# Block-sparse attention into a gated feed-forward: common keys of two query blocks in one 64-column product, two units to a batch, and batch loads issued by GpSimd

## The chip, the cores and the metric

The kernel runs on one core of a Trainium2 chip. The metric is the device time of one execution in microseconds (us), smaller is better. Before the change, three runs took 306.48, 301.97 and 305.78 us; the median is 305.78 us.

The engines are named as the profile names them: PE is TensorE (matrix products), PEld its weight loads, DVE is VectorE, ACT ScalarE, POOL GpSimd, SP SyncE (which only issues DMAs here). SPq and POOLq are their instruction queues.

## The reference: what is computed

Four batches, eight heads, 768 positions, head dimension 64. The positions form 24 blocks of 32. A query block attends to itself and its two neighbours, to the first and the last block, and to three blocks drawn by a table; the first and the last query block attend to everything. The result goes, 512 wide, through a root-mean-square norm and a gated feed-forward of inner width 1536:

```python
mask = np.abs(blk_i - blk_j) <= window              # window = 1, blocks of 32
mask = mask | (blk_i == 0) | (blk_j == 0) | (blk_i == n_blocks - 1) | (blk_j == n_blocks - 1)
for qb in range(n_blocks):
    for kb in sampled_blocks[qb]:
        mask[qb * block:(qb + 1) * block, kb * block:(kb + 1) * block] = True
scores = np.where(mask, scale * q @ k.T, -1e9)
attn = softmax(scores)                              # over the keys
x = (attn @ v), heads side by side                  # 3072 x 512
xn = x / sqrt(mean(x * x) + 1e-6) * rms_g
out = (silu(xn @ w_gate) * (xn @ w_val)) @ w_out    # 512 -> 1536 -> 512
```

## The kernel before

**Tiles and units.** The 3072 rows are 24 tiles of 128 rows, six to a batch. The first batch is computed densely (all 768 keys for every query, with the mask added through 24 more rows of the contraction: `dk`, `dexp`, `dav`). The other three batches are sparse: a tile is four query blocks of 32, and of each block only the keys that it attends to are gathered. Tile 5 (`AT`) of a sparse batch holds the first and the last block, which attend to everything, and two ordinary blocks. The tiles of a batch are grouped into units (`UNITS`, L63, from `SPLIT`, L62): a unit goes through the feed-forward together, with 128 columns for each of its tiles. Batch 0 has units of 1, 1, 1 and 3 tiles, batch 1 of 1, 2, 1, 2, batch 2 of 1, 2, 3, and batch 3 of 3, 3; these are 13 units.

**A sparse batch.** K, Q and V come in from DRAM as float32, in two halves of 768 KB each (`load_kv`, L439-444), into one of three raw buffers (`RAWS`, pool `raw`). They are cast to bfloat16 (`fill_k`, `fill_v`, on whichever of POOL, DVE, ACT the planner takes from `CE`, L819), K and Q are transposed by PE (`turn`, L464) and copied out by ACT (`turned`). V is stored to a table of rows in DRAM (`store_v`, L473), and the blocks that a tile needs are read back from it: fixed ones by SP (`pair_v`, L533-541), sampled ones, whose addresses are in registers, by SP for two of the three draws and by POOL for the third (`block_v`, L517). Sampled blocks of K are copied within the chip (`kg_sampled`, L507, by POOL; its time stands at L153, 198 copies).

Of a tile, four heads at a time (a "run"), PE computes scores (`qk`, L562, in row tiles of 64 x 128; `qka`, L578, for tile 5), ACT the exponential (L568, L585), PE the product of probabilities and V (`av`, matmul at L611), DVE the division by the sum, which is a 65th column of V (`xo`, L621-622).

**The product in question (`av`, L589-614).** The probabilities lie keys-by-queries, so they are the weights of the matmul, and 65 columns of V stream past. Keys come in groups of 128. For each head of an ordinary tile each of the four query blocks has 128 keys of its own (`vg[:, 0..3]`), and two neighbouring blocks share another 128 (`vg[:, 4]` and `vg[:, 5]`). Every product is 32 weight columns wide and stands in one of four column tiles of the array (`tile_position=(0, 32 * i)`, tile size 128 x 32), which write 32 partitions each. An ordinary run has 4 heads of 8 products, 32 in all. For tile 5 the first two blocks have six groups of 128 keys in common, and the other two have two groups each: 16 products a head, 64 a run. There are 30 ordinary runs and 6 runs of tile 5; this is 1344 products.

**After attention.** A sum of squares (`sq`, L638, DVE), the inverse root (`rsq`, L647-649, POOL), the scaling (`xq`, L656, DVE), a transposition: by PE and a copy for the first seven units (`tr` L667 and `cp`, `NPET` in L51), by a transposing DMA of SP for the rest (`xt`, L678). Then, in parts of 384 or 512 columns, gate product (`proj`, L691, G below), tanh (`th`, L700, ACT), DVE (`uu`, L706), value product (L691 with `wv`, V below), DVE (`hp`, L717), and at last the output product (`yy`, L730, Y below) with its copy (`yo`) and store (`so`).

**Weights and loads at the start.** The weights come by POOL's DMAs with a cast (`load_w` L254, `load_wo` L258), in four parts of gate and value and two of the output. The loads of batches 1 to 3 are issued by SP, in a fixed sequence; those of K of batch 1 wait in SP's queue until parts 2 and 3 of the value weights have landed (`gate_sync`, L261, called in `lkv`, L939).

**What sets the order.** All instructions are issued by a planner inside the kernel (L1154-1247): every operation has a cost on each engine that may do it, dependencies, buffers it takes and releases, and a priority; the planner steps through time, takes the operation that could start first, and writes it to its engine. Each engine executes its own list strictly in that order. So constants (`FP`, `KFP`, `KDP`, `SQP`, `CPV`, `DLAT`, and the lists of engines `CE`, `SQE`, `CPE`) change the order everywhere. The planner's cost of a run of `av` is 12 x 0.0315 us (L1017), 28 x 0.0315 us for tile 5.

Of the kernel before, what the change touches and what calls it, by code (L numbers as in the profile page):

```python
# [17 lines left out]
def kernel(  # L18
# [19 lines left out]
    P = 128  # L38
    B, H, S, D = q.shape
    NB = S // 32  # L40
    NC = S // P
# [10 lines left out]
    NSLOT, NAUG, NOPEN, NDB = 5, 2, 2, 1  # L52
    IXAT, RGAT = 36.0, 48.0
    NPT, NKG, NVG, NRAW = 5, 2, 4, 3
    AHEAD, HURRY, HURU = 0.2, ("av", "xo", "sq", "rsq", "xq", "tr", "cp"), 0
    NSTARV, ZPAT, NG2 = 3, 32.0, 20
    AH = {"uu": 0.3, "hp": 0.3, "th": 0.3}
    WARM = (11, 10, 2)
    HD, NT3 = NC * D // 2, 3
    VE = ("SP", "SP", "POOL")  # L60
    LP = {(x, b) for x in "" for b in (1, 2, 3)}
    SPLIT = (((5,), (0,1), (2,),( 3, 4)), ((5,), (0, 1), (2, 3, 4)), ((5, 0, 1), (2, 3, 4)))  # L62
    UNITS = [(0, 0, 1), (0, 1, 1), (0, 2, 1), (0, 3, 3)]  # L63
    ND = len(UNITS)
    for b in range(NDB, B):
# [103 lines left out]
    def idle(n, bk=7):  # L169
# [7 lines left out]
        out=kmask, in_=kmask, compare_op=ALU.is_ge, fill=0.0,  # L177
        base=0, pattern=[[1, NC], [-32, NB]], channel_multiplier=NC)
    nc.gpsimd.affine_select(
        out=kmask, in_=kmask, compare_op=ALU.is_ge, fill=0.0,  # L180
        base=31, pattern=[[-1, NC], [32, NB]], channel_multiplier=-NC)
    nc.gpsimd.affine_select(
        out=ident, in_=ident, compare_op=ALU.not_equal, fill=1.0,
        base=0, pattern=[[-1, P]], channel_multiplier=1)
    nc.gpsimd.affine_select(
        out=Bm, in_=Bm, compare_op=ALU.is_ge, fill=0.0,
        base=1, pattern=[[-1, 32]], channel_multiplier=1)
    nc.gpsimd.affine_select(
        out=Bm, in_=Bm, compare_op=ALU.is_ge, fill=0.0,
        base=1, pattern=[[1, 32]], channel_multiplier=-1)  # L190
    nc.gpsimd.affine_select(
        out=Bm, in_=Bm, compare_op=ALU.not_equal, fill=1.0,
# [13 lines left out]
    for t in aug:  # L206
# [7 lines left out]
        out=eq[0:NB], in0=jb[0:NB], in1=samp_f[0:NB].unsqueeze(2).to_broadcast([NB, NRND, 32]),  # L214
# [4 lines left out]
    for r in range(NRND):  # L219
        nc.vector.tensor_tensor(  # L220
            out=Bm[0:NB], in0=Bm[0:NB], in1=eq[0:NB, r], op=ALU.max)
    nc.vector.tensor_scalar(
        out=Bneg, in0=Bm, scalar1=-MASKV, scalar2=MASKV, op0=ALU.mult, op1=ALU.add)
    qm = PS[:, 2, 0:NC * NB].rearrange("p (c j) -> p c j", j=NB)
    for c in range(NC):
        nc.tensor.matmul(
            out=qm[:, c, :], lhsT=Kind[0:NB, c, :], rhs=Bneg[0:NB, 0:NB], start=True, stop=True)
# [3 lines left out]
        out=aug[0][:, 1, :, 0, 0:D], in_=A[0][:, 1, :, 0:D])  # L231
# [277 lines left out]
    globs, kglob, vaugs = {}, {}, {}  # L509
# [79 lines left out]
    def av(b, n, pp, bk):  # L589
        p_ = [pts.pop((b, n, 2 * pp + i)) for i in range(2)] if n == AT else pts.pop((b, n, pp))  # L590
        vg = vgs[b, n]
        o_ = PS[:, bk[0], 0:4 * (D + 1)].rearrange("p (a d) -> p a d", a=4)
        tiles["o", b, n, pp] = o_
        begun = set()
        for a in range(4):
            hd = slice((4 * pp + a) * (D + 1), (4 * pp + a + 1) * (D + 1))
            w = []
            if n == AT:
                p1 = p_[a // 2][:, a % 2]
                for m in range(NC):  # L600
                    w += [(i, p1[:, 64 * m + 32 * i:64 * m + 32 * i + 32], vaugs[b][:, m, 4 * pp + a, :]) for i in range(2)]
                    if m < 2:
                        lo = 64 * NC + 64 * m
                        w += [(i, p1[:, lo + 32 * (i - 2):lo + 32 * (i - 1)], vg[:, (i, 5)[m], hd]) for i in (2, 3)]
            else:
                p1 = p_[:, a % 2, a // 2]
                w += [(i, p1[:, 32 * i:32 * i + 32], vg[:, i, hd]) for i in range(4)]
                w += [(i, p1[:, P + 32 * i:P + 32 * i + 32], vg[:, 4 + i // 2, hd]) for i in range(4)]
            last = {i: k_ for k_, (i, _, _) in enumerate(w)}
            for k_, (i, l_, r_) in enumerate(w):  # L610
                nc.tensor.matmul(  # L611
                    out=o_[32 * i:32 * i + 32, a, :], lhsT=l_, rhs=r_, start=i not in begun, stop=k_ == last[i],
                    tile_position=(0, 32 * i), skip_group_check=True)
                begun.add(i)

    def xo(u, t, pp):
        b, ns, nt = UNITS[u]
# [154 lines left out]
    banks[2] = 5.1  # L772
    S_, S3, TP1 = [(0, 1), (2, 3)], [(0, 1), (2, 3), (4, 5)], [(6,), (5,), (4,)]
    LAT = {"PE": 0.2, "ACT": 0.16, "DVE": 0.08, "POOL": 0.1, "DMA": 1.9, "DMA2": 2.0, "SP": 2.0, "GD": 2.2, "GQ": 2.5}
    DLAT = {"turnk": 3.0, "turnq": 3.0, "st": 2.5, "l": 4.0, "lq": 4.0, "cp": 2.2, "pvi": 3.0, "gd": 2.2}
    ALT = {"g": [(6,)], "y": [(7,)], "av": [(6,)]}
    SPM, RING = 1.0, 6.0
    ops, end, made = [], {}, {}
# [24 lines left out]
    for g, i in ((2, 0), (2, 1), (3, 0), (3, 1), (0, 2), (1, 2), (2, 2), (3, 2)):  # L803
# [3 lines left out]
        out=gB, in_=moe_rms_g.unsqueeze(0).to_broadcast([P, DM])))  # L807
# [2 lines left out]
        load_q2()  # L810

    WOG, ORD = None, "vkq"
    FP, QP3, SQP = 0.5, 2.5, 0.4
    KDV, LIC, PLI = 0.48, 1.5, 0
    GVC, GVP, GWP, GPC = 0.46, 0.5, 3.5, 0.52
    CPV, CPK, KFP, KDP = 1, 1, 1.1, 1.1
    D_, A_, P_ = {"DVE": 0.62}, {"ACT": 0.86}, {"POOL": 1.0}
    DA_, DP_, AP_, DAP_ = {**D_, **A_}, {**D_, **P_}, {**A_, **P_}, {**D_, **A_, **P_}
    CE = {1: (DP_, DP_, DP_), 2: (P_, P_, P_), 3: (DAP_,DAP_,DAP_)}  # L819
    KFE, SQE, YOE = ("DVE",), ("DVE", ), ("DVE", "ACT")  # L820
    TTE, TTP = ("ACT",), -1
    KDE, CPE = ("POOL",), ("ACT",)
    prev = None
    for i in range(NWC + NOC):
        for m in range(2 if i < NWC else 1):
# [33 lines left out]
        out=aug[1][:, 1, :, :, D:KQ], in_=aug[0][:, 1, :, :, D:KQ]), at=5.1)  # L859
    for g in range(NP):  # L860
# [12 lines left out]
        for i in range(2):  # L873
            for n_, (es, lo, hi) in enumerate((KP, QP)[i][g == 0]):
                m_ = len(es) * (hi - lo)
                if i == 0:
                    pri = (-1, g, 0.5 + 0.1 * n_ + (g == 0 and lo == 3))
                else:
# [4 lines left out]
                   pri, lambda e, p, a=(g, i, es, lo, hi): tpx(*a, p),  # L883
# [6 lines left out]
                elif g == 0 and lo == 0:  # L890
                    de.update(ac)
                op(("ev",) + key[1:], de, [key], pri,
                   lambda e, p, a=(g, i, es, lo, hi): evx(*a, e), [], [(None, key)])
# [24 lines left out]
    for e_ in REGS:  # L918
        for part, (w_, lo, hi) in enumerate(REGS[e_]):
            op(("rg", e_, part), {e_: {"POOL": 2.7, "ACT": 2.0, "SP": 1.5, "DVE": 2.7}[e_]}, [("ix", 5)], (6, part),  # L920
               lambda e, p, a=(e_, part): table_regs(*a), at=RGAT + (7.0 * part if e_ == "ACT" else 0.0))
# [9 lines left out]
    for b in range(NDB, B):  # L931
        for i in (0, 1, 2):
            for hf in range(2):
                key = ("kvq"[i], b, hf)
                if key[:2] in LP:
                    continue
# [14 lines left out]
        for hf in range(2):  # L951
            for c in range(2):
                op(("sfv", b, hf, c), ce[0], [("l", "v", b, hf), ("on",) if b == NDB else ("on", 1)], (CPV, b, 0),
                   lambda e, p, a=(b, hf, c): fill_v(*a, e), [("va", b)], [("raw", ("v", b, hf))])
                for i, x in enumerate("kq"):
                    op((("sfk", "sfq")[i], b, hf, c), ce[1 + i], [("l", x, b, hf)] + (tp0[i] if b == NDB else []), (CPK, b, 1 + i),
                       lambda e, p, a=(b, x, hf, c): fill_k(*a, e), [(x + "row", b)], [("raw", (x, b, hf))])
        fv = [("sfv", b, hf, c) for hf in range(2) for c in range(2)]
        op(("st", b), {"SP": 0.8}, fv + [("lt",)], (-1, b), lambda e, p, b=b: store_v(b), d=2.6)
        for x in "kq":  # L960
            for j in range(2):
                op(("tt" + x, b, j), {"PE": 12 * 0.056}, [("sf" + x, b, j, c) for c in range(2)], (TTP, b, j),
                   lambda e, p, a=(b, x, j): turn(*a, p), [(S_, ("tt" + x, b, j)), (x.upper() + "T", b)], [(x + "row", b)])
                op(("turn" + x, b, j), pick_({"ACT": 2.75, "DVE": 2.75}, TTE), [("tt" + x, b, j)], (-0.5, b, j),
                   lambda e, p, a=(b, x, j): turned(*a, e), [], [(None, ("tt" + x, b, j))])
# [58 lines left out]
    for u, (b, c0, nt) in enumerate(UNITS):  # L1024
        w = nt * P
        if b < NDB:
            w, last = nt * P, c0 + nt == NC
            ng = NC // JT[nt]
            for pr in range(NP):
# [3 lines left out]
                for g in range(ng):  # L1033
# [12 lines left out]
                   lambda e, p, a=(u, pr): dav(*a, p), [([(7,)] + [(6,)] * (u < 3), ("o", u, pr)), ("xo", u)],  # L1046
# [4 lines left out]
                   lambda e, p, a=(u, pr): dxo(*a), [], [(None, ("o", u, pr))])  # L1051
# [13 lines left out]
        for t in range(nt):  # L1065
            op(("xq", u, t), {"DVE": 0.75}, [("rsq", u), ("lg",)], (SQP, u, t),
               lambda e, p, a=(u, t): xq(*a), [("xq", u)],
# [11 lines left out]
        for f in range(NF // fg):  # L1079
            n_ = fg * w  # L1080
            op(("g", u, f), {"PE": fg * NP * mm(w)}, [("cp", u), ("w", w_of[f])], (4, u, f, 1),
               lambda e, p, a=(u, f): proj(*a, wg, "gp", p), [([(4,)] + [(6,)] * (2 < u < NG2), ("g", u, f)), ("hp", HG[u])])
            op(("th", u, f), {"ACT": 0.12 + n_ / 1200.0}, [("g", u, f)], (FP, u, f),
               lambda e, p, a=(u, f): th(*a), [("th", (u, f))])
            op(("uu", u, f), {"DVE": 0.155 + n_ / 960.0}, [("th", u, f)], (FP, u, f),
               lambda e, p, a=(u, f): uu(*a), [("uu", (u, f))],
               [(None, ("g", u, f)), ("th", (u, f))])
            op(("v", u, f), {"PE": fg * NP * mm(w)}, [("g", u, f)], (4, u, f, 0),
               lambda e, p, a=(u, f): proj(*a, wv, "vp", p), [([(5,)], ("v", u, f))],
               [("xn", u)] if f == NF // fg - 1 else [])  # L1090
            op(("hp", u, f), {"DVE": 0.155 + n_ / 960.0}, [("uu", u, f), ("v", u, f)], (FP, u, f),
               lambda e, p, a=(u, f): hp(*a), [],
               [(None, ("v", u, f)), ("uu", (u, f))])
        for t in range(nt):
            nh = 2 if u == NU - 1 and t == nt - 1 else 1
            for h in range(nh):
                for k_ in range(4):
# [3 lines left out]
                       lambda e, p, a=(u, t, 4 * h + k_): yy(*a, p),  # L1101
# [3 lines left out]
                   lambda e, p, a=(u, t, h): yo(*a, e), [("yo", (u, t, h))], [(None, ("y", u, t, h))])  # L1105
                op(("so", u, t, h), {"SP": 0.5 if b < NDB or c0[t] != AT else 1.5}, [("yo", u, t, h)], (0, u, t),
                   lambda e, p, a=(u, t, h): so(*a), [], [("yo", (u, t, h))], d=0.8 / nh)
# [46 lines left out]
    while ready:  # L1154
        pick = None
        for o in ready:
# [8 lines left out]
            for e in o["engs"]:  # L1165
                t1 = max(got[0] + (SPM if e == "SP" and o["key"] not in in_seq0 else 0.0), free[e])
                k_ = o["key"]
# [9 lines left out]
        _, o, e, t1, got = pick  # L1177
# [17 lines left out]
        k_ = o["key"]  # L1195
# [82 lines left out]
```

## Time and profile before

| | |
|---|---|
| profiled execution: its own time | 302.08 us |
| its span, first to last instruction | 300.5 us |
| granted TensorE clock, mean | 0.988 |
| PE busy | 279.2 us, 4605 matmul records |
| DVE, ACT, POOL busy | 203.6, 170.5, 134.3 us |
| DMA moved | 47.94 MB, mean 160 GB/s |

The profile gives, of one execution, the busy time of each engine, the chain of work that ended last (followed back from the last instruction: at each step to what released it), groups of instructions by source line, and the waits. A timeline view merges neighbouring instructions of one kind: start, time from the first start to the last end, what, and how many. PE's matmuls are pipelined, so the ends overlap the next start; the pace of PE is read from start to start. Some matmul records are missing (the products of L611 have 1312 records of 1344).

### The profile page before, as it was taken

The page shows a single profiled execution, that of the slowest core. Times are in us where ns is not written, and L with a number is a line of the kernel's source. Part 1 is how long each engine was busy: PE and PEld are TensorE (multiplying, and loading weights), DVE is VectorE, ACT ScalarE, POOL GpSimd, SP SyncE. Part 2 cuts the span into 40 slices and gives each one's busy share as a digit, 9 for nine tenths or more (in the row PEclk, how much of TensorE's full clock was granted, in tenths as well). Part 3 has the DMA queues.
Part 4 walks back from the last instruction along what each step waited for, and adds up shares of the span by engine and source line. Part 5 has one row for each costly group of instructions (what it writes and reads, how often), then busy time and mean ns, then how long its engine had stood idle before and what let it go on. Part 6 is the DMA issues. An engine that isn't in the chain of part 4 may idle for free.

```text
span 300.5 us, 11870 instructions
## 1 busy us (share of the span) xinstructions
PE 279.2 (93%) x4605; PEld 198.3 (66%) x4631; DVE 203.6 (68%) x511; ACT 170.5 (57%) x222; POOL 134.3 (45%) x345
## 2 busy tenths in 40 slices
PE   8999799999879999799989979999999979999995
PEld 7898588856446777577867657875655446545553
DVE  5788567686628976696578755865577758855742
ACT  5999577649935455587743544688862453302320
POOL 3559000439637627869684802487386300100000
PEclk9999999999979999999999997999999999999999
DMA  6999998199733459965724569997425380032002
GB/s 193 366 246 226 232 215 169 27 347 242 199 68 74 100 166 340 364 120 153 122 55 116 140 122 349 312 241 174 125 58 136 101 177 4 1 95 63 2 35 105
DMA packets 57494, 47.94 MB, mean 160 GB/s; under 512 B 14141, under 2 KB 52542, under 8 KB 57438
## 3 DMA queue, kind: packets, MB, share of 16 engines
q1 hardware_dynamic: 49226, 40.20, 49.2%
q0 software_dynamic: 7904, 6.92, 13.3%
q8 instruction: 36, 0.59, 0.8%
q14 instruction: 20, 0.16, 0.2%
q10 hardware_dynamic: 308, 0.07, 0.1%
HBM read 41.15 MB, written 8.89 MB: 167 GB/s over the span
## 4 chain that ended last, share of the span: by engine, by line
PE 66%; DMA 15%; SPq 8%; issue 5%; DVE 2%; ACT 1%; POOL 1%; POOLq 0%; ACTq 0%
PE PS L691 33%; PE PS L730 18%; SPq L517 7%; DMA wv<-in_moe_w_val_dram 4%; PE PS L611 4%; PE PS L308 4%; DMA xn<-xq 4%; PE PS L562 2%; DMA RAWC<-in_v_dram 2%; DMA VXC<-vrows 2%; PE PS L343 2%; PE PS L464 2%; DMA RAWC<-in_k_dram 2%; PE PS L287 1%; SPq L758 1%
## 5 line engine op out<-in xcount | busy, mean ns | idle before, releaser
L691 PE MATMUL PS<-xn,wg 128*128 128x128 bf16 (+2 forms) x624 | 75.1, 266 | 5.5 <-DMA xn<-xq 2.0
L700 ACT ACTIVATE th<-PS 128x384 bf16<-128x384 f32 (+1 forms) x90 | 46.0, 518 | 58.2 <-PE PS L691 48.9
L691 PE MATMUL PS<-xn,wv 128*128 128x128 bf16 (+2 forms) x624 | 77.1, 266 | 2.1 <-issue 0.9
L706 DVE SCALAR_TENSOR_TENSOR uu<-th,PS 128x384 bf16<-128x384 bf16 (+1 forms) x90 | 51.8, 578 | 29.0 <-ACT th L700 27.1
L730 PE MATMUL PS<-wo,hp 128*128 128x512 bf16 (+1 forms) x274 | 66.5, 373 | 1.8 <-issue 0.8
L717 DVE TENSOR_TENSOR hp<-uu,PS 128x384 bf16<-128x384 bf16 (+1 forms) x90 | 51.2, 578 | 23.1 <-PE PS L691 21.8
L691 PEld LDWEIGHTS <-wg 128*128 128x128 bf16 x624 | 49.7, 99 | 23.1 <-issue 4.6
L153 POOL COPY XC<-XC 128x128 bf16 x198 | 51.1, 303 | 30.2 <-PE PS L578 13.9
L691 PEld LDWEIGHTS <-wv 128*128 128x128 bf16 x624 | 48.5, 98 | 19.9 <-issue 2.7
L730 PEld LDWEIGHTS <-hp 128*128 128x128 bf16 x300 | 28.1, 98 | 24.0 <-issue 0.3
L329 ACT ACTIVATE PTC<-PS 128x768 bf16<-128x768 f32 x44 | 33.3, 816 | 5.4 <-PE PS L308 5.0
L568 ACT ACTIVATE PTC<-PS 128x1024 bf16<-128x1024 f32 x24 | 24.1, 1024 | 7.3 <-PE PS L562 7.2
L151 ACT COPY XC<-PS 128x1536 bf16<-128x1536 bf16 (+1 forms) x9 | 22.4, 2493 | 7.3 <-PE PS L464 6.5
L740 ACT ACTIVATE yo<-PS 128x512 f32<-128x512 f32 x12 | 7.2, 597 | 27.5 <-PE PS L730 19.0
L308 PE MATMUL PS<-XC 88*128 88x128 bf16 (+1 forms) x192 | 21.4, 245 | 0.4 <-ACT PTC L329 0.4
L656 DVE SCALAR_TENSOR_TENSOR xq<-XO,rs,gB 128x512 bf16<-128x512 f32 x24 | 19.9, 853 | 0.3 <-POOL rs L649 0.2
L742 DVE TENSOR_SCALAR yo<-PS 128x512 f32<-128x512 f32 (+1 forms) x13 | 8.4, 648 | 16.5 <-PE PS L730 15.8
L611 PEld LDWEIGHTS <-PTC 128*32 128x32 bf16 x1056 | 12.3, 97 | 10.1 <-issue 6.5
L153 POOL CAST RAWC<-RAWC 128x768 bf16<-128x768 f32 x5 | 4.2, 837 | 33.0 <-DVE RAWC L155 21.2
L153 POOL CAST AUG<-RAWC 128x768 bf16<-128x768 f32 (+2 forms) x19 | 15.2, 812 | 6.9 <-DMA RAWC<-in_k_dram 3.2
L517 POOL DMA_DIRECT2D PTC<-vrows x34 | 17.4, 515 | 1.6 <-PE PS L691 0.4
L517 POOL DMA_DIRECT2D VXC<-vrows x32 | 16.7, 525 | 2.8 <-DMA vrows<-RAWC 1.8
(113 smaller groups left out, 312.3 us busy)
## 6 DMA issues: line engine op xcount, KB each, us to landing
out_dram<-yo SPq DMA_DIRECT2D x20, 256.0 KB, 2.5
RAWC<-in_v_dram SPq DMA_DIRECT2D x6, 768.0 KB
RAWC<-in_k_dram SPq DMA_DIRECT2D x6, 768.0 KB, 9.1
RAWC<-in_q_dram SPq DMA_DIRECT2D x6, 768.0 KB, 7.5
PTC<-vrows SPq DMA_DIRECT2D x68, 32.5 KB, 1.9
VXC<-vrows SPq DMA_DIRECT2D x64, 32.5 KB, 2.1
VXC<-vrows SPq DMA_DIRECT2D x30, 65.0 KB, 4.0
PTC<-vrows SPq DMA_DIRECT2D x30, 65.0 KB, 2.9
```

The lines of the kernel that those rows point to most:

```text
L151: nc.scalar.copy(out=out, in_=in_)
L153: nc.gpsimd.tensor_copy(out=out, in_=in_)
L308: nc.tensor.matmul(out=s_[:, e, j * w:(j + 1) * w], lhsT=x[0:KQ, 0, e, jt * P:(jt + 1) * P], rhs=x[0:KQ, 1, e, c0 * P:c0 * P + w], start=T ...
L329: nc.scalar.activation(out=pts[u, pr][:, g * kt:(g + 1) * kt].rearrange("p j e w -> p e j w"), in_=s_[:, :, 0:kt * w].rearrange("p e (j w) ...
L517: ENG[VE[r]].dma_start(out=new_vg(g, n)[32 * r:32 * r + 32, x, :].bitcast(U8), in_=vrows[g].rearrange("r f -> (r f)").bitcast(U8)[bass.ds( ...
L568: nc.scalar.activation(out=t_.rearrange("p h l x -> p (h l x)"), in_=tiles.pop(("s", b, n, pp)).rearrange("p h l x -> p (h l x)"), func=AF ...
L611: nc.tensor.matmul(out=o_[32 * i:32 * i + 32, a, :], lhsT=l_, rhs=r_, start=i not in begun, stop=k_ == last[i], tile_position=(0, 32 * i), ...
L691: nc.tensor.matmul(out=p_[:, j, :].rearrange("p (t w) -> p t w", w=P), lhsT=w_[:, c, f_ * P:(f_ + 1) * P], rhs=xns[u][:, :, c, :], start=( ...
L700: nc.scalar.activation(out=t_, in_=tiles["gp", u, f], func=AF.Tanh, scale=0.5)
L706: nc.vector.scalar_tensor_tensor(out=t_, in0=tiles.pop(("th", u, f)), scalar=1.0, in1=tiles.pop(("gp", u, f)), op0=ALU.add, op1=ALU.mult)
L717: nc.vector.tensor_tensor(out=hps[u][:, f * fg:(f + 1) * fg, :], in0=tiles.pop(("uu", u, f)), in1=tiles.pop(("vp", u, f)), op=ALU.mult)
L730: nc.tensor.matmul(out=tiles["yp", u, t, h], lhsT=hps[u][:, f, t * P:(t + 1) * P], rhs=wo[:, f, x], start=(f == 0), stop=(f == NF - 1))
```

## The change

- `av` (L600-614): where two neighbouring query blocks share a group of keys, their two products of 32 weight columns become one of 64, in a column tile of 64 (tile size 128 x 64) that writes 64 partitions. Products that belong to one block stay 32 wide. A head of an ordinary tile has four of 32, then two of 64; a head of tile 5 has, in order, one of 64, two of 32, two of 64, four of 64. A run is 24 products (36 for tile 5), all in all 936: 528 of 32 and 408 of 64.
- Units: every sparse batch is cut into (5, 0, 1) and (2, 3, 4). There are 10 units. Feed-forward products number 960 at L691 (1248 before) with the same columns in sum. The first seven units are transposed after the norm by PE as before, which is now 60 transposes (40 before), and three units by DMA (six before).
- Loads of K, Q, V of batches 1 to 3 (`LP`): 18 DMAs of 768 KB go from SP's queue to POOL's, the first after the first half of the output weights; each waits there for a raw buffer. The two gates in SP's queue go with them.
- Planner constants: allowed engines and priorities. In the order that results, 14 of the 21 sums of squares over a whole row are on ACT, 4 of the 7 copies after PE transposes are on DVE (all 7 were on ACT), and 9 casts of K and Q leave POOL, 8 of them for DVE.

```diff
-    AHEAD, HURRY, HURU = 0.2, ("av", "xo", "sq", "rsq", "xq", "tr", "cp"), 0
+    AHEAD, HURRY, HURU = 0.8, ("av", "xo", "sq", "rsq", "xq", "tr", "cp"), 0
...
-    LP = {(x, b) for x in "" for b in (1, 2, 3)}
-    SPLIT = (((5,), (0,1), (2,),( 3, 4)), ((5,), (0, 1), (2, 3, 4)), ((5, 0, 1), (2, 3, 4)))
+    LP = {(x, b) for x in "vkq" for b in (1,2,3)}
+    SPLIT = (((5,0,1), (2, 3, 4)), ((5, 0, 1), (2, 3, 4)), ((5, 0, 1), (2, 3, 4)))
...
                 p1 = p_[a // 2][:, a % 2]
                 for m in range(NC):
-                    w += [(i, p1[:, 64 * m + 32 * i:64 * m + 32 * i + 32], vaugs[b][:, m, 4 * pp + a, :]) for i in range(2)]
-                    if m < 2:
-                        lo = 64 * NC + 64 * m
-                        w += [(i, p1[:, lo + 32 * (i - 2):lo + 32 * (i - 1)], vg[:, (i, 5)[m], hd]) for i in (2, 3)]
+                    w.append((0, 2, p1[:, 64 * m:64 * m + 64], vaugs[b][:, m, 4 * pp + a, :]))
+                    if m == 0:
+                        w += [(i, 1, p1[:, 64 * NC + 32 * (i - 2):64 * NC + 32 * (i - 1)], vg[:, i, hd]) for i in (2, 3)]
+                    elif m == 1:
+                        w.append((2, 2, p1[:, 64 * NC + 64:64 * NC + 128], vg[:, 5, hd]))
             else:
                 p1 = p_[:, a % 2, a // 2]
-                w += [(i, p1[:, 32 * i:32 * i + 32], vg[:, i, hd]) for i in range(4)]
-                w += [(i, p1[:, P + 32 * i:P + 32 * i + 32], vg[:, 4 + i // 2, hd]) for i in range(4)]
-            last = {i: k_ for k_, (i, _, _) in enumerate(w)}
-            for k_, (i, l_, r_) in enumerate(w):
+                w += [(i, 1, p1[:, 32 * i:32 * i + 32], vg[:, i, hd]) for i in range(4)]
+                w += [(2 * x, 2, p1[:, P + 64 * x:P + 64 * x + 64], vg[:, 4 + x, hd]) for x in range(2)]
+            last = {i + y: k_ for k_, (i, m_, _, _) in enumerate(w) for y in range(m_)}
+            for k_, (i, m_, l_, r_) in enumerate(w):
                 nc.tensor.matmul(
-                    out=o_[32 * i:32 * i + 32, a, :], lhsT=l_, rhs=r_, start=i not in begun, stop=k_ == last[i],
+                    out=o_[32 * i:32 * (i + m_), a, :], lhsT=l_, rhs=r_, start=i not in begun, stop=k_ in last.values(),
                     tile_position=(0, 32 * i), skip_group_check=True)
-                begun.add(i)
+                begun.update(range(i, i + m_))
...
-    DLAT = {"turnk": 3.0, "turnq": 3.0, "st": 2.5, "l": 4.0, "lq": 4.0, "cp": 2.2, "pvi": 3.0, "gd": 2.2}
+    DLAT = {"turnk": 3.0, "turnq": 3.0, "st": 2.5, "l": 4.0, "lq": 4.0, "cp": 2.2, "pvi": 5.0, "gd": 2.2}
...
-    FP, QP3, SQP = 0.5, 2.5, 0.4
-    KDV, LIC, PLI = 0.48, 1.5, 0
+    FP, QP3, SQP = 2, 2.5, 0.6
+    KDV, LIC, PLI = 0.48, 1.2, 0
...
-    CPV, CPK, KFP, KDP = 1, 1, 1.1, 1.1
+    CPV, CPK, KFP, KDP = 4,4,0.3,2
...
-    CE = {1: (DP_, DP_, DP_), 2: (P_, P_, P_), 3: (DAP_,DAP_,DAP_)}
-    KFE, SQE, YOE = ("DVE",), ("DVE", ), ("DVE", "ACT")
+    CE = {1: (D_,DA_,DA_), 2: (P_,D_,D_), 3: (DP_,DP_,P_)}
+    KFE, SQE, YOE = ("DVE",), ("DVE", "ACT"), ("DVE", "ACT")
...
-    KDE, CPE = ("POOL",), ("ACT",)
+    KDE, CPE = ("POOL", ), ("DVE", "ACT")
```

The lines of the changed kernel from here on stand one lower: the product of probabilities and V is L612 there.

## The prediction

> **What bounds the kernel now.** I read the page's table of busy time and its chain first.
>
> ```profile
> PE 279.2 (93%) x4605; PEld 198.3 (66%) x4631; DVE 203.6 (68%) x511; ACT 170.5 (57%) x222; POOL 134.3 (45%) x345
> ...
> PE 66%; DMA 15%; SPq 8%; issue 5%; DVE 2%; ACT 1%; POOL 1%; POOLq 0%; ACTq 0%
> ```
>
> PE is busy 279.2 of 300.5 us, and two thirds of the chain is PE; no other engine passes 68%. So work that is added to PE is paid nearly in full, and what is saved elsewhere buys only PE's idle time, 21.3 us. Where that lies is told by the table of stretches.
>
> ```profile
> 80.00:250.00 170.00, 157.64 (x3212) 110.93 (x3230) 116.04 (x280) 96.68 (x115) 95.92 (x266) 0.98 0.63 162
> 0.00:80.00 80.00, 74.61 (x1096) 60.86 (x1102) 58.22 (x174) 61.29 (x83) 37.21 (x78) 1.00 0.95 226
> 250.00:300.50 50.50, 46.92 (x301) 26.49 (x301) 29.38 (x59) 12.57 (x25) 1.12 (x2) 0.99 0.14 45
> ```
>
> The second number is PE: in 80 to 250 us, where the sparse batches' attention runs, it is idle for 170 - 157.64 = 12.4 us. The waits of PE name what for.
>
> ```profile
> PE PS L611 <- DMA VXC<-vrows: 3.9, 3, 3.1
> PE PS L691 <- issue: 2.3, 2, 1.4
> PE PS L691 <- DMA xn<-xq: 2.0, 2, 1.7
> PE PS L691 <- DMA wg<-in_moe_w_gate_dram: 1.8, 1, 1.8
> ...
> PE PS L691 <- DMA wv<-in_moe_w_val_dram: 0.8, 1, 0.8
> ```
>
> They are single waits for transfers, the longest 3.1 us; no engine holds PE up regularly.
>
> **How PE spends a run of the changed product.** This is the timeline of PE in 168 to 175 us (start, length, what, count); I read it from start to start.
>
> ```profile
> 170.60 0.59 PE L730 MATMUL PS<-wo,hp 128*128 128x512 bf16 x2
> 171.13 0.43 PE L611 MATMUL PS<-PTC 128*32 128x65 bf16 x32
> 171.49 0.49 PE L562 MATMUL PS<-XC 64*128 64x32 bf16 x24
> 171.92 0.84 PE L691 MATMUL PS<-xn,wv 128*128 128x128 bf16 x12
> 172.69 0.43 PE L611 MATMUL PS<-PTC 128*32 128x65 bf16 x32
> 173.05 0.49 PE L562 MATMUL PS<-XC 64*128 64x32 bf16 x24
> ```
>
> A run of 32 products of 32 columns takes 0.36 us to the next kind of work (171.13 to 171.49, and 172.69 to 173.05). Single starts show why: four products, one for each column tile, start within 10 ns, and the next four some 30 ns later, so a run is 8 rounds. Between kinds there is something more. At 171.92, 12 products of L691 last 0.77 us; 12 transposes of the same array size (66.40 to 67.07 us, followed by Y, also 128 x 128) last 0.67, which is 12 x 0.056. The 0.10 that is over stands where the tile size goes from 128 x 128 to 128 x 32. The last product of L611 to the first of L562 is 0.125 to 0.127 us in every such place, a round being 0.03; from L562 on to L691 it is 0.119 against 0.025 inside. Between kinds of one tile size (L667 to L730, L464 to L691) nothing is over. So **a change of tile size costs PE 0.095 us**, in each of the pairs that this trace has: 128 x 128, 64 x 128 and 128 x 32. Then a run's 0.36 us are 8 rounds of 0.033 and one change at its end. A run of tile 5 (148.10 to 148.94 us) is 0.84 us: without the change 0.745, that is 6 rounds of 0.031 for each of 4 heads.
>
> **The change, part by part.**
>
> *64 columns instead of 32.* The two halves of a shared group already stand in the same round, side by side: four 32s fill a round, and so do two 64s. The merge saves no round. At best it saves the starts of 408 products; by the run's own rate (8 x 0.033 / 32 = 0.008 us a product) that is 3.3 us. It adds changes between tile sizes 128 x 32 and 128 x 64. An ordinary run goes 32, 64, 32, 64 ... over four heads: 7 changes inside. A run of tile 5 goes 64, 32, 64 in each head: 8 changes; and it takes 7 rounds instead of 6, as the second two blocks' first products no longer lie beside a product of the first two: 4 x 0.03 = 0.12 us. The trace has no change between 32 and 64 columns. Bounds: 0 (they may count as one kind, both being column tiles; then a gain up to 3.3 us remains) and 0.095, the figure of every pair seen. I take 0.095, since 128 x 32 against 128 x 128 too differs in columns alone. Sum: 30 x 7 x 0.095 = 20.0, plus 6 x (8 x 0.095 + 0.12) = 5.3; **+25.3 us of PE**. Low end -3.3.
>
> On tile sizes the Trainium skill (TensorEngine Tiling (Array Packing), Key Properties) says that changing the tiling mode, not just the tile, drains TensorE; it lists 128 x 64 and 128 x 32 as separate modes. The 0.095 us agree for the pairs that the trace has; by that rule the sum is the one just made.
>
> *Wider units.* L691 at 128 columns goes at 0.056 us (above), at 256 at 0.109 (196.92 us: 8 in 0.87), at 384 at 0.162 (75.66 to 76.95: 8 in 1.29). Before: 576 x 0.056 + 288 x 0.109 + 384 x 0.162 = 125.9. After: 288 x 0.056 + 672 x 0.162 = 125.0. **-0.9 us.** Twenty more transposes on PE: +1.1. Changes of tile size between kinds of work are 117 before and 113 after in the orders: -0.4. Together -0.2.
>
> *Other engines.* DVE: 24 more `uu` and `hp` each of 0.55 us for 18 of 0.685 (+0.9 each), 12 more casts at 0.55 to 0.60 (+7), four copies after transposes (some +3, by ACT's 0.60 and 1.44), 14 squares gone (-11 at 0.704 + 0.081): 203.6 to about 204. ACT gains the squares, 14 at 0.60 (a 512-wide th) to 0.85: some +6 to 177. POOL: nine casts fewer (-7.9), 18 DMA issues more at 0.82 (row of L254): +15; about 140 of 300. All lie beside PE. If the order were bad this cover would be gone in places; I bound that by the idle time that the same engines leave now, +-6 us.
>
> *Loads from POOL.* Two waits of PE for weights (1.8 and 0.8) stand at 34 and 38 us; SP's loads of V of batch 1 were issued at 19.8, among the weights. Now they come behind the first half of the output weights in one queue; up to -2.6 us. K of batch 1, issued at 38.8 and 57.2 behind the gates, is no later. The wait for a raw buffer is now in POOL's list: behind it are the copies of sampled K (198 at 0.303 us), the sampled V of the third draw (0.52 each) and the roots of the norm, and PE waits for all three. In SP's queue these waits for buffers (L442 on ACT, DVE and POOL casts, and q) come to 13.6 us in sum, 2.4 at most. Bounds -2.6 to +13.6; I take 0, since PE's rows of waits do not hold a raw load today and the planner places each load when it has a buffer free.
>
> *What is late next.* 25 us more on PE in stretches where it idles 12.4 us: part of the idle time is waiting for a transfer or an engine that now gets its time. I let 40% of it, 5 us, be taken up (between 0 and 12.4).
>
> **Sum**, against the execution profiled (302.1 us; its span and 1.6 around it): 302.1 + 25.3 - 0.2 - 5 = 322. This execution is 3.7 us under the median of the three runs, beside the lowest; against the median it would be 326. I predict **322 us**, with 310 to 334 as this case's own range (idle time taken up wholly, 315, and a good or bad order, +-6; the runs' spread).
>
> **Rivals.**
>
> 1. *Change between 32 and 64 free* (not slower). For it: both are column tiles, in the same quarters of the array. Against: 128 x 32 to 128 x 128 and to 64 x 128 cost the same 0.095, as if any difference counted. Then 302.1 - 0.2 + 0.7 (the seventh rounds) = 302.6, up to 3.3 less for fewer starts and 2.6 less at the weights: **300 us** (295 to 308 with the order). It decides at about 0.02 us a change: 258 changes are then 5 us. Chance 0.20.
> 2. *Price by count.* The Trainium skill (TensorEngine Tiling (Array Packing), Instruction Overhead) gives each matmul about 60 cycles at least; by that 408 fewer would save, as an estimate, 408 x 25 ns = 10 us. As a mechanism here it is bounded by the row: 32 products in 8 rounds of 0.033 us is 0.008 each, so products in different column tiles do not pay singly, and it is the 3.3 us of rival 1. Alone, at 302 - 3.3 = 299 us, it has 0.05 of rival 1's 0.20.
> 3. *Half price*: only one direction drains, or the next weights are loaded early: 302.1 + 12.6 - 0.2 - 3 = **311 us**. Chance 0.06.
> 4. *POOL's queue late*: the changes cost 0.095, and the 13.6 us of waits for buffers stand in front of the copies of K, of which PE sees most: 322 + 11 = **333 us** (328 to 345). For it: POOL is at 9 tenths busy in slices of the middle already; against: it has 5 us in 10 free on average. Chance 0.14.
>
> **Chances.** Forecast 0.60, rival 1 0.20, rival 3 0.06, rival 4 0.14. The range 298 to 337 holds the forecast (0.58), rival 3, most of rival 4 (0.10) and half of rival 1: about 0.83. What a measurement tells from no change is about 2%, 6 us: under 300 is faster, over 312 slower (from the median). Slower: 0.57 + 0.14 + 0.03 = 0.74. Faster: 0.09, of rival 1. Within: 0.17.
>
> **What would show it.** In the changed timeline a run of 24 should take about 8 x 0.033 + 8 x 0.095 = 1.0 us to the next kind (0.36 now), starts going 30, 125, 125 ns by turns; tile 5's 36 products 1.7 us (0.84 now). PE should be busy some 300 us, idle in the middle 7 to 12. A run of 0.3 us would make rival 1 true. POOL's waits for raw buffers with PE's waits on sampled K behind them would be rival 4. Waits for weights at 34 and 38 us should be gone.

## The result, and the profile after

Four runs of the changed kernel took 325.05 to 327.27 us, median 327.01 (a fifth took 326.19), against 304.09 for four runs of the kernel before. The ratio is 1.0735 (95% interval 1.0643 to 1.0827): slower by 7%. Executions that took over 1.5% longer than the fastest of their kernel stand in the medians of this document but not in its ratios, so a ratio is not always the quotient of two medians. The forecast was 322 us, and the prediction names two ranges, 310 to 334 and 298 to 337; 327.0 lies in both. The profiled execution took 325.05 us with a span of 323.4, which is 22.9 more than the span before.

The page's table of busy time, its chain, and the chain by line, all of the changed kernel:

```profile
PE 307.4 (95%) x3931; PEld 202.4 (63%) x3962; DVE 206.3 (64%) x511; ACT 176.7 (55%) x250; POOL 140.8 (44%) x347
...
PE 82%; DMA 7%; DVE 4%; issue 2%; ACT 2%; SPq 1%; POOL 0%; POOLq 0%; ACTq 0%
PE PS L692 37%; PE PS L731 17%; PE PS L612 15%; PE PS L562 4%; DMA VXC<-vrows 3%; PE PS L308 3%; DMA PTC<-vrows 2%; PE PS L343 2%; PE PS L464 2%; DMA RAWC<-in_k_dram 1%; ACT PTC L329 1%; PE PS L287 1%; PE PS L578 1%; PE PS L668 1%; DVE hp L718 1%
```

PE has fewer instructions and is busy 28.2 us longer (307.4 against 279.2). The chain is PE for 82% instead of 66%, and the line of the changed product (L612; L611 before) is 15% of it, where it had 4%. DVE, ACT and POOL are busy 2.7 to 6.5 us longer. The chain by line of the kernel before, for comparison:

```profile
PE PS L691 33%; PE PS L730 18%; SPq L517 7%; DMA wv<-in_moe_w_val_dram 4%; PE PS L611 4%; PE PS L308 4%; DMA xn<-xq 4%; PE PS L562 2%; DMA RAWC<-in_v_dram 2%; DMA VXC<-vrows 2%; PE PS L343 2%; PE PS L464 2%; DMA RAWC<-in_k_dram 2%; PE PS L287 1%; SPq L758 1%
```

The table of stretches and the waits of PE:

```profile
80.00:250.00 170.00, 164.09 (x2358) 102.67 (x2382) 104.94 (x252) 94.81 (x128) 101.76 (x268) 0.97 0.54 143
```

```profile
PE PS L612 <- DMA VXC<-vrows: 5.3, 1, 5.3
PE PS L692 <- DVE hp L718: 2.3, 4, 1.2
PE PS L171 <- DVE zt L158: 1.2, 1, 1.2
...
PE PS L692 <- DVE uu L707: 0.5, 1, 0.5
```

In 80 to 250 us PE is idle for 5.9 us, where it had 12.4. Over the span it is 323.4 - 307.4 = 16.0, where it had 21.3. The waits for weights (L691 on `wg` and `wv`) and for transposed rows are gone. The waits for V blocks (5.3 against 3.9) and for `hp` of DVE (2.3 against 0.2) are some 2 us longer each. Nothing new of any size holds PE up; it has more to do.

What it has to do shows in its timeline, two runs of the product and what follows each:

```profile
93.47 1.25 PE L612 MATMUL PS<-PTC 128*32 128x65 bf16 x24
94.66 0.82 PE L692 MATMUL PS<-xn,wg 128*128 128x384 bf16 x4
...
95.83 1.25 PE L612 MATMUL PS<-PTC,RAWC 128*32 128x65 bf16 x24
97.02 0.49 PE L562 MATMUL PS<-VXC,XC 64*128 64x32 bf16 x24
```

From start to start a run of 24 is 1.19 us; the run of 32 was 0.36. (The view gives both widths the shape of the first.) The single starts of the first head and a half of that run, in ns, with the columns of the product and the time since the product before:

```
93474  32          93618  64  +134     93769  32  +148     93912  64  +133
93477  32   +3     93621  64    +3     93772  32    +3     93916  64    +4
93481  32   +4                         93776  32    +4
93484  32   +3                         93779  32    +3
```

Products side by side in different column tiles start 3 to 4 ns apart, as before. In the ordinary runs of the kernel before, a round starts 30 ns after the start of the round before it (median); here the next round comes 134 ns after the last product of 32 columns and 148 ns after the last of 64. The weight loads (PEld) show the same break. Within one width, the weights of a round's first product start to load some 30 ns ahead of it (median 28 ns in the kernel before, 31 to 32 here); across a change of width they start 2 ns ahead of it (median of all changes). So the next weights are not loaded ahead across a change. Whether it is this, or the array emptying first, that takes the time, these records do not separate.

The two widths add to the same columns of PSUM (the memory that PE writes its sums to), but that is not what costs. From 64 to 32 columns the next head begins with columns of its own, and the change costs no less; and in tile 5 successive 64-column products that add to the same columns start 29 to 36 ns apart. Over all runs the median from first start to the next kind of work is 1.184 us (0.362 before); where no wait falls into it, tile 5's takes 1.895 us (0.836 before). On PE that is 30 x 0.822 + 6 x 1.06 = 31.0 us.

### The profile page after: what moved, and what is told of

Read it like the earlier page. It is cut to its first block, busy times and chain, and to the rows that moved or that the text cites. A ratio compares the mean times of both kernels' runs of the same rounds, so it can differ in the third digit from the quotient of the medians.

```text
span 323.4 us, 10543 instructions
## 1 busy us (share of the span) xinstructions
PE 307.4 (95%) x3931; PEld 202.4 (63%) x3962; DVE 206.3 (64%) x511; ACT 176.7 (55%) x250; POOL 140.8 (44%) x347
## 4 chain that ended last, share of the span: by engine, by line
PE 82%; DMA 7%; DVE 4%; issue 2%; ACT 2%; SPq 1%; POOL 0%; POOLq 0%; ACTq 0%
PE PS L692 37%; PE PS L731 17%; PE PS L612 15%; PE PS L562 4%; DMA VXC<-vrows 3%; PE PS L308 3%; DMA PTC<-vrows 2%; PE PS L343 2%; PE PS L464 2%; DMA RAWC<-in_k_dram 1%; ACT PTC L329 1%; PE PS L287 1%; PE PS L578 1%; PE PS L668 1%; DVE hp L718 1%
## 5 line engine op out<-in xcount | busy, mean ns | idle before, releaser
L701 ACT ACTIVATE th<-PS 128x384 bf16<-128x384 f32 x96 | 46.9, 496 | 64.8 <-PE PS L692 53.6
L692 PE MATMUL PS<-xn,wv 128*128 128x384 bf16 (+1 forms) x480 | 77.3, 296 | 2.3 <-DVE hp L718 2.3
L692 PE MATMUL PS<-xn,wg 128*128 128x384 bf16 (+1 forms) x480 | 74.6, 296 | 0.7 <-DVE uu L707 0.5
L718 DVE TENSOR_TENSOR hp<-uu,PS 128x384 bf16<-128x384 bf16 x96 | 51.9, 551 | 33.5 <-PE PS L692 33.1
L707 DVE SCALAR_TENSOR_TENSOR uu<-th,PS 128x384 bf16<-128x384 bf16 x96 | 52.2, 551 | 19.3 <-ACT th L701 16.0
L692 PEld LDWEIGHTS <-wg 128*128 128x128 bf16 x480 | 40.9, 98 | 23.6 <-issue 1.2
L692 PEld LDWEIGHTS <-wv 128*128 128x128 bf16 x480 | 39.8, 98 | 24.9 <-issue 3.7
L612 PEld LDWEIGHTS <-PTC 128*32 128x32 bf16 (+1 forms) x738 | 28.3, 100 | 17.8 <-issue 6.9
L612 PE MATMUL PS<-PTC 128*32 128x65 bf16 (+1 forms) x366 | 19.9, 207 | 0.0
L612 PE MATMUL PS<-VXC,PTC 128*32 128x65 bf16 (+1 forms) x300 | 18.2, 210 | 0.0
```

The source lines that it names most:

```text
L612: nc.tensor.matmul(out=o_[32 * i:32 * (i + m_), a, :], lhsT=l_, rhs=r_, start=i not in begun, stop=k_ in last.values(), tile_position=(0, ...
L692: nc.tensor.matmul(out=p_[:, j, :].rearrange("p (t w) -> p t w", w=P), lhsT=w_[:, c, f_ * P:(f_ + 1) * P], rhs=xns[u][:, :, c, :], start=( ...
L701: nc.scalar.activation(out=t_, in_=tiles["gp", u, f], func=AF.Tanh, scale=0.5)
L707: nc.vector.scalar_tensor_tensor(out=t_, in0=tiles.pop(("th", u, f)), scalar=1.0, in1=tiles.pop(("gp", u, f)), op0=ALU.add, op1=ALU.mult)
L718: nc.vector.tensor_tensor(out=hps[u][:, f * fg:(f + 1) * fg, :], in0=tiles.pop(("uu", u, f)), in1=tiles.pop(("vp", u, f)), op=ALU.mult)
```

## The experiments

Theory D is the one of the prediction: each change between column tiles of 32 and of 64 drains PE (it has to run empty before it goes on; the runs show what a change costs, not that PE runs empty). The first four ran on one chip, beside the kernel before (305.52 us). Where the order of instructions is kept, only the products of `av` differ; DVE, ACT, POOL and SP then have the same lists, instruction for instruction.

**1. The changed kernel with 32-column products.**

```diff
-  (the changed loop of av: one 64-column product for two blocks' common keys)
+                    w += [(i, p1[:, 64 * m + 32 * i:64 * m + 32 * i + 32], vaugs[b][:, m, 4 * pp + a, :]) for i in range(2)]
...
+                w += [(i, p1[:, P + 32 * i:P + 32 * i + 32], vg[:, 4 + i // 2, hd]) for i in range(4)]
```

> The changed kernel (its units, loads and order, instruction for instruction) with the products of probabilities and V as they were before: 32 columns each, 8 rounds a run. Theory D (each change between column tiles of 32 and of 64 drains PE): a run falls from 1.18 to 0.36 us and one of tile 5 from 1.90 to 0.84, which is 31 us of PE; part of it comes back as waits, so 296 to 306 us. Rival P (the new order, units or loads cost the time, the merge is nearly free): 322 to 328 us.

Measured: 306.8 us, ratio to before 0.991 (0.980 to 1.003). So new units, new loads and a new order, all together, cost nothing that can be measured (at most 0.3% by the interval). Rival P falls.

**2. The kernel before with the merged products**, its order kept; the edit is the hunk of `av` in the diff of the change, alone.

> The kernel before, its order instruction for instruction, with only the merged 64-column products. Theory D: 31 us more on PE, less what PE's idle time takes up (0 to 12): 322 to 336 us. Rival P: 300 to 308 us.

Measured: 331.0 us, ratio 1.084 (1.076 to 1.093). The merge costs the same in either order: here 8.4%, and in the changed one 8.3% (1.0735 against 0.991). PE is busy 312.6 us, 33.4 more than in the kernel before, at a mean granted clock of 0.969 against 0.988, and its idle time falls from 21.3 to 15.8 us.

**3 and 4. The same merged products, sorted by width** over all four heads of a run, or over two heads at a time:

```diff
+        w.sort(key=lambda x: (x[0] // 4, x[2]))     # head // 4, width; fourth experiment: x[0] // 2
```

(`w` collects the products of all four heads first, each with its head; start and stop marks go with it.)

> The changed kernel with the same 24 (36) products in another order: in a run first the 32-column products of all four heads, then all the 64-column ones. One change inside a run instead of 7 (8). Theory D: a run takes 8 rounds and two changes, about 0.50 us, tile 5's 28 products of a head group in 7 rounds each about 1.1: about 29 us less PE work than changed, 298 to 310 us. Rival W (a 64-column product is slow in itself, by its 64 weight columns, whatever stands beside it): a run stays above 1.0 us, 322 to 328 us.

> As the one before, but grouped by two heads: 3 changes inside a run instead of 7 (8). Theory D, in proportion to the changes at 0.114 us each: a run about 0.36 + 0.03 + 3 x 0.114 = 0.73 us, tile 5's about 1.3; 308 to 318 us. Rival W: a run above 1.0 us, 322 to 328 us.

Measured: 303.26 us (0.991; 0.984 to 0.997) grouped by four, 311.58 us (1.022; 1.014 to 1.030) grouped by two. Timeline of PE, a run and what follows it: products of 32 columns (first experiment), grouped by four (third), by two (fourth).

```profile
91.94 0.43 PE L611 MATMUL PS<-PTC 128*32 128x65 bf16 x32
92.30 0.82 PE L691 MATMUL PS<-xn,wg 128*128 128x384 bf16 x4
```

```profile
93.91 0.57 PE L613 MATMUL PS<-PTC 128*32 128x65 bf16 x24
94.41 0.82 PE L693 MATMUL PS<-xn,wg 128*128 128x384 bf16 x4
```

```profile
94.18 0.79 PE L613 MATMUL PS<-PTC 128*32 128x65 bf16 x24
94.91 0.82 PE L693 MATMUL PS<-xn,wg 128*128 128x384 bf16 x4
```

A run is 0.36, 0.50 and 0.73 us, and 1.19 in the changed kernel. The last three have the same 24 products, weights and columns; only how often the width changes differs. In one table (changes counted inside the 36 runs):

| | changes | a run, us | PE busy, us | PE idle, us | median, us | ratio to before |
|---|---|---|---|---|---|---|
| 32 columns only | 0 | 0.36 | 279.3 | 24.3 | 306.8 | 0.991 |
| sorted over four heads | 36 | 0.50 | 282.2 | 19.4 | 303.3 | 0.991 |
| sorted over two heads | 108 | 0.73 | 291.6 | 21.8 | 311.6 | 1.022 |
| as changed | 258 | 1.18 | 307.4 | 16.0 | 327.0 | 1.074 |

From 36 to 258 changes PE's busy time grows by 25.2 us, 0.113 a change, and the time by 23.7, 0.107 a change (by the ratios some 25 us; the last row was measured apart from the first three, beside 304.09 us for the kernel before). That is theory D; rival W, slow 64-column products as such, falls with the third experiment.

The price also depends on how soon the change before lies back. Where a width has run for two rounds or more, the next product comes 127 to 128 ns after the last one, in the third and fourth experiments and from 32 to 64 as from 64 to 32, and 128 to 131 ns on the way to `proj` or `qk`, where it was 127 in the kernel before. Where only one round lies between two changes, as in an ordinary run of the changed kernel, it is 134 and 148 ns, and 150 on the way out. The first round of 64 columns after a change is also the slow one: in the third experiment the round behind it starts 49 ns after its last product, later ones 31. So the dearer change lies in going on after a single round, not in leaving 64 columns.

The Trainium skill's rule (TensorEngine Tiling (Array Packing), Key Properties: changing the mode drains, changing the tile does not) agrees with these rows, for 128 x 32 against 128 x 64 too: a change of width costs 0.11 us, one of the tile alone 3 to 4 ns. That page's overhead of about 60 cycles for each matmul (Instruction Overhead) is not paid product by product in different column tiles: a round of two products of 64 columns takes 35 ns in the third experiment, one of four of 32 columns 30 ns in the kernel before (medians of the ordinary runs, start to start).

**5 and 6. The changed kernel with 32-column products and one other part undone**, planned again: loads by SP (`LP` empty), or the units of before (`SPLIT`).

> The changed kernel with 32-column products (as the first experiment) and with the loads of batches 1 to 3 given back to SP with their gates; units and constants as changed, the order planned for it. My theory: where the loads are issued is off the path; 300 to 308 us, equal to the first experiment, apart from 2 to 3 us of waits for weights that come back at 34 to 38 us. Rival (POOL's list delayed by waits for raw buffers): 5 us or more faster than the first experiment.

> The changed kernel with 32-column products and with the units of the kernel before (13 units); loads by POOL and constants as changed, the order planned for it. My theory: the columns of the feed-forward are the same, some 1 us more on PE; 300 to 310 us. Rival (three-tile units feed PE better or worse): 6 us or more away from the first experiment, either way.

Measured: 312.65 us (1.037; 1.030 to 1.044) and 314.26 us (1.045; 1.038 to 1.053), both outside what I expected. PE's busy time is 283.5 and 280.6 us, 4.2 and 1.3 more than in the first experiment, at a mean granted clock of 0.967 and 0.961 against 0.978; its idle time grew by 3.2 and 6.5, to 27.5 and 30.8 us. In the sixth, PE waits 14.4 us in four waits for transposed rows, which the first experiment does not have:

```profile
PE PS L691 <- DMA xn<-xq: 14.4, 4, 10.0
PE PS L611 <- DMA PTC<-vrows: 5.5, 1, 5.5
```

Each edit makes the planner choose another order for all engines, so these two runs do not show what the loads or units cost, only that an order with one setting exchanged comes out 4 to 5% above the kernel before. That the sixth has the size of its rival (6 us or more away) decides nothing either, for the same reason.

**7 and 8. Fewer changes between kinds of work.** The planner counts a change of tile size as a delay of PE's next operation (0.2 us with the products sorted over four heads, 0.1 us with 32-column products):

```diff
+                if e == "PE" and shape(o["key"]) != now[0]:
+                    t1 += 0.2
...
-                op(("av", u, t, pp), {"PE": na * 0.0315}, ...
+                op(("av", u, t, pp), {"PE": na * 0.0315 - 0.1}, ...
```

(`qk` likewise, 0.1 less. `shape` tells row tiles, column tiles and the full array apart.)

> The grouped products (third experiment), and the planner told of changes of tile size: an operation of PE whose tile size differs from the last one's is taken to start 0.2 us later, so work of one kind is put together. Changes between kinds of work fall from 113 to 77. Theory D: 36 x 0.12 us less PE work, 4 us; half or more of it in the time: 297 to 302 us. Rival: runs put together come later for DVE and ACT, and PE waits as much as it saves: 303 to 308 us.

> The same with 32-column products (first experiment) and 0.1 us: changes between kinds fall from 113 to 79. Theory D: 34 x 0.1 us = 3.4 us less PE work: 298 to 305 us; rival as before: 304 to 309 us.

Measured: 340.26 us (1.127; 1.120 to 1.134) and 351.32 us (1.167; 1.160 to 1.173). Both far beyond even the rival. The stretch from 80 to 250 us of the seventh and of the eighth:

```profile
80.00:250.00 170.00, 147.76 (x2257) 92.74 (x2272) 105.60 (x248) 93.22 (x123) 92.82 (x248) 0.86 0.50 136
```

```profile
80.00:250.00 170.00, 138.39 (x2503) 85.99 (x2519) 102.39 (x242) 88.49 (x117) 93.10 (x254) 0.87 0.49 136
```

PE is idle there for 22.2 and 31.6 us, and its granted clock is 0.86 and 0.87, against 0.96 in the first experiment: the stretch does less work and PE works slower in it. The fall is not even: in the seventh the granted clock is 0.50 from 115 to 132 us, from 166 to 176 and from 238 to 251, and 1.00 between. Some 4 us of changes were saved, and by the ratios 41 and 53 us lost. Against the third experiment, the span of the seventh is 39.4 us longer: 22.6 of it is idle time of PE (42.0 against 19.4), and 16.8 is busy time (299.0 against 282.2), although PE has the same products and fewer changes. For the eighth against the first experiment these are 31.1 and 12.2 us. The largest waits of PE are for transposed rows in both (10.2 and 11.6 us, in two waits). My reading is that work of one kind put together leaves PE with nothing between the steps of the other chains; no run here tests it.

**9. The order before, with merged products sorted over four heads.**

> The kernel before, its order instruction for instruction, with the merged products grouped over four heads (one change inside a run). Theory D: against the second experiment (331 us) the 6 changes inside an ordinary run and 7 inside one of tile 5 go; against the kernel before there remain 30 x 0.14 + 6 x 0.16 = 5 us of PE: 303 to 310 us. Rival (the 64-column products cost more in this order): above 314 us.

Measured: 300.79 us against 302.44, ratio 0.994 (0.989 to 0.998). Below what I expected. The runs do take 0.50 us instead of 0.36, and PE is busy 286.8 us in its profiled execution (302.86 us, 2.1 above the median), 7.6 more than before. Its idle time is 14.5 instead of 21.3, and this takes up 6.8 of the 7.6.

**10. The changed kernel, and the planner told the true cost.**

```diff
-                op(("av", u, t, pp), {"PE": na * 0.0315}, ...
+                op(("av", u, t, pp), {"PE": 1.89 if n == AT else 1.18}, ...
```

> The changed kernel, alternating products, and the planner told what they cost: 1.18 us for a run and 1.89 for tile 5 (in place of 0.38 and 0.88), the order planned anew. Theory D: the 31 us stay on PE, which is busy 95% already; 318 to 328 us. Rival (the loss comes from an order planned for runs three times shorter): under 315 us.

Measured: 327.27 us (1.087; 1.078 to 1.096), the changed kernel's time to 0.3 us, and by the ratios no better than it (1.0735; 1.0643 to 1.0827). PE is busy 309.8 us. The loss is not that of an order planned with a wrong price.

**11 and 12. Who issues the loads, every other list kept.** In the first experiment's kernel the 18 loads go to SP at the same point of the plan, in the kernel before to POOL:

```diff
-        (nc.gpsimd if key[:2] in LP else nc.sync).dma_start(
+        nc.sync.dma_start(        # eleventh; nc.gpsimd in the twelfth
```

> The first experiment (changed kernel, 32-column products) with every engine's list as it is, except that the 18 loads of batches 1 to 3 stand in SP's list instead of POOL's, at the same point of the plan. My theory: it does not matter who issues a load, 299 to 309 us, within 2% of the first experiment. Rival: their waits for a raw buffer (29 us in POOL's list of the changed kernel) now stand ahead of SP's reads of V blocks, PE waits for those: 310 us or more.

> The kernel before with only those 18 loads moved from SP's list to POOL's, at the same point of the plan; SP's gates stay. My theory: within 2% of the kernel before, 299 to 309 us. Rival: the waits for buffers stand ahead of the copies of sampled K, PE waits for them: 310 us or more.

Measured: 309.87 us against 302.77 (1.024; 1.017 to 1.031), and 306.25 against 302.77 (four runs, 302.09 to 310.51, too scattered for an interval; no difference is shown). The eleventh is 0.9 us outside what I expected and 0.1 short of the rival; by the ratios it is 3% above the first experiment (1.024 against 0.991, measured on two chips). In it PE waits for the gate weights again, three times:

```profile
PE PS L611 <- DMA VXC<-vrows: 5.6, 1, 5.6
PE PS L691 <- DMA wg<-in_moe_w_gate_dram: 4.9, 3, 2.6
```

In the first experiment there is no such wait. So in the changed order, with no gates in SP's queue, it is worth something that the loads stand behind the weights in one queue: 4.9 us of waits for weights, and a span 6.6 us longer without it, 4.1 of them idle time of PE (28.4 against 24.3). The rival's mechanism, V blocks late behind SP's waits for buffers, is not seen: the waits for V blocks (5.6, and 1.3 for the other buffer) are no longer than the first experiment's (9.4 and 1.1).

## Why the prediction was right

**What bounds the kernel.** PE, as said. Work added to PE was paid for: 28.2 us more busy, 22.9 us more span.

**64 columns: the term that decides.** That the merge saves no round is shown by the third experiment: without the alternation a run still goes in 8 rounds, those of 64 columns no shorter than those of 32 (35 against 30 ns), and the kernel is not faster than the first experiment. That a change between 32 and 64 columns costs like the other changes was the choice between 0 and 0.095 us a change; it was right, a little low. By the measure that the prediction took (0.125 - 0.03), the starts give 134 - 30 = 104 ns after 32 columns and 148 - 30 = 118 ns after 64, and the table gives 0.113. The 0.095 holds for a change that stands alone, 127 - 30 = 97 ns; it was read from such changes, and inside an ordinary run of the changed kernel there are none: only one round lies between two changes, and that makes each dearer. Leaving the run from a single round of 64 columns also takes longer, 0.150 against 0.127 us. An ordinary run took 1.18 us where the prediction had 1.0, and tile 5's 1.895 where it had 1.7, so the sum is 31.0 us instead of 25.3. This mis-sized term is the largest error.

**What idle time takes up.** I let 5 us of it be taken up, between 0 and 12.4; from before to changed it fell by 5.3 (21.3 to 16.0), between the first experiment and the changed kernel, which have the same order, by 8.3, and in the second experiment by 5.5. In the ninth, 7.6 us more on PE disappeared nearly whole, into 6.8 us of idle time. From the first experiment to the fourth, 12.3 us more on PE took up 2.5. So idle time took up 2.5 to 8.3 us of additions of 8 to 33 us, and never all 21 to 24 that there were. In the stretch from 80 to 250 us 5.9 us stayed idle, under the 7 to 12 of the prediction. 31.0 - 0.2 - 5.3 is 25.5, and the span grew by 22.9. The rest lies in PE's busy time, which grew by 28.2 and not by 31 (the prediction had PE busy some 300 us; it was 307.4). In the second experiment, with the same products in the order before, it grew by 33.4. Its ends are modelled and the granted clock differs between executions, and I leave these differences open.

**Luck in the number.** Of the 5.0 us between 322 and 327.0, 2.0 are the starting point, 302.1 of one execution against the median of 304.09. The rise was forecast as 20 and came to 22.9: the changes cost 5.7 us more than forecast, and 2.6 us of the sum did not appear in the span. That these two partly cancel is luck.

**Wider units.** With 32-column products PE is busy 279.3 us in the new order and 279.2 in the old: the -0.2 us stands. What wider units alone do to the waits was not shown.

**Other engines.** DVE 206.3, ACT 176.7 and POOL 140.8 us, where I had about 204, 177 and 140. They lie beside PE.

**Loads from POOL.** Taken as 0, between -2.6 and +13.6. The waits for weights went, as allowed for. The price that I feared was mis-sized but harmless. These are the largest waits of POOL for a raw buffer in the changed kernel:

```profile
POOL RAWC L442 <- DVE RAWC L155: 11.1, 2, 10.2
...
POOL RAWC L442 <- DVE ms L639: 8.1, 1, 8.1
...
POOL RAWC L442 <- DVE rz L355: 4.2, 1, 4.2
```

With the smaller ones they come to 29.1 us, twice the 13.6 that I took from SP's queue. Yet PE's list of waits has none at `qk` (L562) that would answer to late copies of K. The eleventh experiment puts the term at a gain in this order, of 7 us by the spans and 10 by the ratios, and the twelfth shows none in the order before; what else in the new order gives that back, so that the first experiment ends level with the kernel before, I could not separate.

**Rivals.** 1 and 2 (a free change, a price by count) are refuted by the table; 3 (half price, one direction only) by the starts, since both directions cost; 4 (POOL late) did not come.

## What to carry to other kernels

Before merging small matmuls, look at their starts: products in different column tiles already run side by side, and a wider one fills the same round. If widths are mixed, sort the products by width, since each change of tile size costs about 0.11 us here, and it is the count of changes that decides, not that of products. Sorting makes the merge harmless, not useful: it gained nothing over the products of 32 columns. And of a cost on a busy engine only a part goes into the engine's idle time: here 2.5 to 8.3 of 21 to 24 us, and the rest was paid.

## What the runs showed of the hardware that I had not expected

- A change of width is dearer when only one round lies between it and the change before: 148 ns from 64 columns and 134 from 32, against 127 to 128 after two rounds or more, and 150 against 128 to 131 ns from 64 columns to another kind of product.
- Across a change of width the next weights are not loaded ahead: their load starts 2 ns before the product, against some 30 ns within one width.
- Sorted over four heads, the merged kernel needs 408 products and 408 weight loads fewer and is no slower than the kernel before in either order (0.991, 0.984 to 0.997; 0.994, 0.989 to 0.998), although PE is busier by 3.0 and 7.6 us. The gain of less than 1% is not shown to be the merge's: with 32-column products the first experiment has 0.991 too.
- Where PE idles 22 to 32 us of 170, its granted clock over that stretch is 0.86 to 0.87 instead of 0.96 to 0.98, so lost time is paid for a second time. The amount of idle time does not set it alone: in the sixth experiment 21.1 us idle go with 0.93. In the seventh it is 0.50 from 166 to 176 us, although no idle time of PE in the ten microseconds before is longer than 1.5 us.
